# A Fourier mixing layer followed by an expert layer with h·cos(h): five changes to the schedule of a tuned one-core kernel

## The chip, the cores and the metric

The program runs on one core of one Trainium2 chip. The metric is device time in microseconds (us) of one execution; several executions of each kernel are timed on the same chip, in rounds, beside executions of the kernel before. The granted TensorE clock (the share of full speed that the chip let TensorE run at, as the trace records it) is given where it matters.

PE is TensorE (PEld its weight loads), DVE is VectorE, ACT is ScalarE, POOL is GpSimd, SP is the engine whose queue issues most DMAs. PSUM is the memory that PE writes its results to, in banks; SBUF is the memory that the engines work from; DRAM is the memory outside the core.

## The reference

```python
def _attn_ref(x):                       # x: (8, 3008, 256) float32
    X = np.fft.fft(x, axis=1)
    X = np.fft.fft(X, axis=2)
    return X.real.astype(np.float32)

def _moe_ref(x, w_in, w_out):           # x: (24064, 256); 256 -> 2048 -> 256
    h = x @ w_in
    g = h * np.cos(h)
    return (g @ w_out).astype(np.float32)
```

Everything is float32. The kernel folds the 256-channel transform into `w_in` (tables Wc and Ws), uses the symmetries of the 3008-row transform, and computes rows k and 3008-k together: with P the cosine part and Q the sine part, one row needs P+Q and the other P-Q.

Of the kernel before, what the change touches and what calls it, by code (L numbers as in the profile page):

```python
# [69 lines left out]

def _row_consts():

    p = np.arange(128)
    neg = SEQ - 5 - 6 * p
    neg[0] = SEQ - 6
    return np.stack([neg, HALF - 5 - 6 * p], axis=1).astype(np.uint32)
# [3 lines left out]
def kernel(  # L80
# [14 lines left out]
    CC_dr = nc.inline_tensor(_chan_consts(), name="chan_mats")  # L95
    IX_dr = nc.inline_tensor(_row_consts(), name="row_table")
# [25 lines left out]
    ix = cpool.tile([128, 2], U32, tag="ix")  # L122
    nc.sync.dma_start(out=ix, in_=IX_dr.ap())

    def load_x(b):
        L = [
            spool.tile([128, 6 * ND], FP, tag=f"xl{j}", bufs=1, name=f"xl{j}")
            for j in range(4)
        ]

        for j in (2, 1):
            nc.gpsimd.indirect_dma_start(
                out=L[j],
                out_offset=None,
                in_=xflat,
                in_offset=bass.IndirectOffsetOnAxis(ap=ix[:, j - 1 : j], axis=0),
                element_offset=b * SEQ * ND,
            )
        nc.gpsimd.dma_start(out=L[1][0:1, 0 : 5 * ND], in_=xrows(b, SEQ - 5, 1, 1, 5))
        nc.gpsimd.dma_start(out=L[1][0:1, 5 * ND :], in_=xrows(b, 0, 1, 1, 1))  # L140
        nc.sync.dma_start(out=L[0], in_=xrows(b, 0, 6, 128))
        nc.sync.dma_start(out=L[3], in_=xrows(b, HALF, 6, 128))
        return L
# [51 lines left out]
    R4 = cpool.tile([128, NB], FP, tag="R4")  # L195
    Rb4 = cpool.tile([128, NB], FP, tag="Rb4")
# [4 lines left out]
    xe_dr = dpool.tile([NB, 2 * 768], FP, tag="xe", name="xe_dr")  # L201
# [25 lines left out]
    def fold_weights():  # L227
# [14 lines left out]
        nc.scalar.dma_start(out=wx_dr, in_=Ws[127:128, :])  # L242
        with nc.allow_non_contiguous_dma(reason="one row to columns"):
            nc.scalar.dma_start(
                out=wex, in_=wx_dr.rearrange("o (f p) -> p (o f)", p=128)
            )
# [7 lines left out]
    def sum_weights():  # L254
        b11, b12 = w2v[:, 0::2, 0:128], w2v[:, 0::2, 128:256]
        b21, b22 = w2v[:, 1::2, 0:128], w2v[:, 1::2, 128:256]
        gtt(WT[0], b12, b11, ALU.subtract)
        gtt(WT[2], b12, b22, ALU.add)
        gtt(WT[1], b11, WT[2], ALU.subtract)
        gtt(WT[3], WT[1], b21, ALU.add)  # L260
# [4 lines left out]
    def fold_x(L, tt, pieces):  # L265

        ops = {}

# [8 lines left out]
        for j in range(4):  # L277
# [5 lines left out]
            if j in (1, 2):  # L283
# [4 lines left out]
                nc.scalar.copy(out=e, in_=s)  # L288
# [3 lines left out]
            O.append(o)  # L292
        for j in (1, 3):
            ops[f"z{j}", 0] = lambda o=O[j]: pin(
                nc.gpsimd.memset(o[:, 6 * 127 :], 0.0)
            )
# [12 lines left out]
        "c1 e1 o1 c3 e3 o3 c0 e0 E0 o0 O0 c2 e2 E2 EO0 EO1 o2 O2 EO2 z1 EO3 z3".split()  # L309
# [92 lines left out]
    def load_ext():  # L402
        X = state["X"] = []
        with nc.allow_non_contiguous_dma(reason="one channel"):
            for tag, row, n in (
                ("e0", 0, 760),
                ("e2", 748, 760),
                ("o0", HALF, 760),
                ("o2", SEQ - 760, 760),
            ):  # L410
                t = spool.tile([128, 768 if tag[0] == "e" else 763], FP, tag=tag, bufs=1, name="x128")
                nc.sync.dma_start(
                    out=t[0:NB, 0:n],
                    in_=bass.AP(
                        tensor=xt,
                        offset=x.offset + row * ND + 128,
                        ap=[[SEQ * ND, NB], [ND, n], [1, 1]],
                    ),
                )
                X.append(t[0:NB])  # L420

    def fold_ext():
        n = RUN + 1
        X = state["X"]
        XA = spool.tile([128, 768], FP, tag="e1", bufs=1, name="XA")[0:NB]
        XG = spool.tile([128, 768], FP, tag="e3", bufs=1, name="XG")[0:NB]

        gtt(XA[:, 1:n], X[0][:, 1:n], X[3][:, 759 : 759 - RUN : -1], ALU.add)
        gtt(XA[:, 0:1], X[0][:, 0:1], X[0][:, 0:1], ALU.add)
        gtt(XG[:, 0:n], X[1][:, 756 : 756 - n : -1], X[2][:, 0:n], ALU.add)  # L430
        ep, em = X[0], X[1]
        gtt(ep[:, 0:n], XA[:, 0:n], XG[:, 0:n], ALU.add)
        gtt(em[:, 0:n], XA[:, 0:n], XG[:, 0:n], ALU.subtract)
        for i, t in enumerate((ep, em)):
            pin(nc.gpsimd.memset(t[:, n:768], 0.0))
            nc.sync.dma_start(out=xe_dr[:, i * 768 : (i + 1) * 768], in_=t[:, 0:768])
        xe = spool.tile([128, 2, NB, 6], FP, tag="xe", bufs=1, name="xe")
        for i in range(2):
            nc.sync.dma_start(
                out=xe[:, i],  # L440
                in_=xe_dr[:, i * 768 : (i + 1) * 768].rearrange(
                    "b (p m) -> p b m", m=6
                ),
            )
# [20 lines left out]
    def dft_ext_out():  # L465
        ps = state["ext"]
        rx = [
            spool.tile([128, 763], FP, tag=t, bufs=1, name="rx")[0:NB]
            for t in ("o0", "o2")
        ]  # L470
        S = []
        for g in range(4):
            n = NO if g > 1 else NE
            t = spool.tile(
                [128, 763 if g % 2 else 768], FP, tag=("e0", "o1", "e2", "o3")[g], bufs=1, name="sx"
            )[0:NB]
            act(t[:, 0:n], ps[32 * g : 32 * g + NB, 0:n])
            S.append(t)
        for kodd in range(2):
            n = NO if kodd else NE  # L480
            a, b = S[2 * kodd][:, 0:n], S[2 * kodd + 1][:, 0:n]
            gtt(rx[kodd][:, 0:n], a, b, ALU.add)
            o = 1 - kodd
            m = n - 2 * o
            gtt(
                rx[kodd][:, RUN - 1 : RUN - 1 - m : -1],
                a[:, o : o + m],
                b[:, o : o + m],
                ALU.subtract,
            )  # L490
            if not kodd:
                gtt(rx[0][:, RUN : RUN + 1], a[:, 0:1], b[:, 0:1], ALU.subtract)
                nc.sync.dma_start(
                    out=r4_dr.rearrange("o b -> b o"), in_=rx[0][:, RUN : RUN + 1]
                )
            nc.sync.dma_start(
                out=r128_dr[:, kodd * RUN : (kodd + 1) * RUN], in_=rx[kodd][:, 0:RUN]
            )
# [101 lines left out]
    def sum_31(i):  # L600
        S = steps[i]
        outer = S.G[:, 0 : 4 * TW].rearrange("p (f c) -> p f c", f=4)[:, 0::3]
        gtt(
            two(blk(S, 4, 2)),
            blk(S, 2).unsqueeze(1).to_broadcast([128, 2, TW]),
            outer,
            ALU.subtract,
        )
# [136 lines left out]
    def middle_tokens():  # L745
        pm = bank("M")
        for f in range(NF):
            mm(pm[:, f * NB : (f + 1) * NB], Wc[:, f * 128 : (f + 1) * 128], R4, True)
        n = NF * NB
        h = spool.tile([128, 3 * n], FP, tag="hm", bufs=1, name="hm")  # L750
        e, r, h = h[:, 0:n], h[:, n : 2 * n], h[:, 2 * n : 3 * n]
        vtt(
            e.rearrange("p (f b) -> p f b", b=NB),
            Rb4.unsqueeze(1).to_broadcast([128, NF, NB]),
            wex.unsqueeze(2).to_broadcast([128, NF, NB]),
            ALU.mult,
        )
        vtt(h, e, pm[:, 0:n], ALU.add)
        act(r.bitcast(I32), h, bias=0.25, scale=1.0)
        vtt(r, h, r.bitcast(I32), ALU.subtract)  # L760
        sin(r)
        times(h, h, r)
        po = bank("M")
        for f in range(NF):
            mm(
                po[0:NB, 0:ND],
                h[:, f * NB : (f + 1) * NB],
                w2[:, f * ND : (f + 1) * ND],
                f == 0,
                f == NF - 1,  # L770
            )
        ob = spool.tile([128, TW], FP, tag="p1", bufs=1, name="p1")
        act(ob[0:NB], po[0:NB, 0:ND])
# [6 lines left out]
            in_=ob[0:NB],  # L780
        )

# [3 lines left out]
    EO, ops = fold_x(L_first, vtt, 1)  # L786
# [5 lines left out]
    fold_now("c0 e0 o0 c3 e3 o3 c2 e2 E2 o2 O2 c1 e1 E0 EO0")  # L792
# [21 lines left out]
    sum_weights()  # L814

# [8 lines left out]
    for i in range(total):  # L824
        t = i * T
        for dt, fn in (
            (-2.2, ext),
# [3 lines left out]
            (3.1, h_minus),  # L831
            (3.7, k_plus),
            (4.3, k_minus),
            (4.4, r_plus),
            (T + 0.2, r_minus),
            (T + 0.21, sin_plus),
            (T + 0.9, g_plus),
            (T + 1.4, sin_minus),
            (T + 2.0, g_minus),
            (T + 2.6, sum_31),  # L840
            (T + 3.8, sum_2),
            (T + 4.4, sum_4),
# [3 lines left out]
            at(t + dt, lambda fn=fn, i=i: fn(i))  # L846
    for q in range(n_tiles):
        t = (8 * q + 9) * T
        for dt, fn in (
            (1.37, comb_copy),  # L850
# [124 lines left out]
```

## The kernel before: what the change touches

The main loop has 376 steps (47 tiles of 256 columns, 8 steps each). In a step PE multiplies P and then adds Q in the same PSUM bank; between the two, ScalarE copies 2P out, so that h_minus = 2P - (P+Q) can be formed. Then come range reduction (k, r), the sine, the product with h, block sums on GpSimd (sums and differences of 128 x 256 blocks of the result G), and seven products with `w_out`, two steps later. Once a tile, VectorE combines the banks of these products, pA to pD (comb and turn, the boundary sums). Each step begins with `ext`: ScalarE writes the share of channel 128, Rb times a column of `wex`, into the bank H, and PE adds P to it. So the first main-loop matmul, H<-Rr,Wc, needs `wex`. Every PE operation is issued by one helper, `mm`, every two-input VectorE operation by `vtt`, every GpSimd one by `gtt`, and every ScalarE activation by `act`, so these share line numbers in the profile, and the reader goes by tile names.

The order of instructions on each engine is fixed by a list of times (T is 4.8):

```python
for dt, fn in ((-2.2, ext), (0.0, mm_P), (0.9, dbl), (2.17, mm_Q),
               (3.1, h_minus), (3.7, k_plus), (4.3, k_minus), (4.4, r_plus),
               (T + 0.2, r_minus), (T + 0.21, sin_plus), (T + 0.9, g_plus),
               (T + 1.4, sin_minus), (T + 2.0, g_minus),
               (T + 2.6, sum_31), (T + 3.8, sum_2), (T + 4.4, sum_4),
               (2 * T + 0.87, mm_X1), (2 * T + 3.04, mm_X2)): ...   # dbl: E <- 2*P
for dt, fn in ((1.37, comb_copy), (2.65, comb_1), (T + 0.25, comb_2), (T + 1.5, comb_22),
               (T + 2.5, comb_3), (2 * T + 2.6, turn_u), (3 * T + 2.6, turn_v)): ...  # once a tile
```

The opening and the batch loads:

```python
# load_x(b), on GpSimd: two gathers, then row 0 of one of them is mended by two more DMAs
nc.gpsimd.dma_start(out=L[1][0:1, 0 : 5 * ND], in_=xrows(b, SEQ - 5, 1, 1, 5))
nc.gpsimd.dma_start(out=L[1][0:1, 5 * ND :], in_=xrows(b, 0, 1, 1, 1))
# fold_weights(), after eight ScalarE copies: the weight row of channel 128 becomes 16 columns, through DRAM
nc.scalar.dma_start(out=wx_dr, in_=Ws[127:128, :])
nc.scalar.dma_start(out=wex, in_=wx_dr.rearrange("o (f p) -> p (o f)", p=128))
# sum_weights(): four GpSimd sums over 128 x 1024, before the main loop
```

Channel 128 of all eight batches takes a path of its own. Four loads of single elements (4 bytes, rows 1 KB apart) go to 8 SBUF rows, GpSimd folds them on 8 partitions, and the result goes through DRAM to get 128 partitions:

```python
nc.sync.dma_start(out=t[0:NB, 0:n], in_=bass.AP(tensor=xt,
    offset=x.offset + row * ND + 128, ap=[[SEQ * ND, NB], [ND, n], [1, 1]]))      # x4
gtt(XA[:, 1:n], X[0][:, 1:n], X[3][:, 759 : 759 - RUN : -1], ALU.add)            # 8 x 752
... [cut: four more such sums, then SBUF -> xe_dr -> xe]
```

The 8 middle rows (k = 1504) are done in one piece near the end, `middle_tokens()`: 16 matmuls with 8 moving columns, range reduction and sine in a chain, 16 matmuls with 8 stationary columns.

## Time and profile before

| | before |
|---|---|
| time, median of 3 (range) | 2113.97 us (2112.97 to 2116.03) |
| PE busy; mean granted clock | 96%; 0.987 |
| first main-loop matmul starts | 59.4 us |
| an undisturbed step | 4.75 us, 22 PE records, 216 ns apart |
| PE lost against that spacing | about 153 us |

The last row is the measure: take the start-to-start distance of consecutive PE matmul records in the trace, subtract what a record of that many columns takes when PE is not held up at full clock (216 ns for 256 columns, 316 ns for 376), and add up what remains. It holds waits, half clock, and weight loads that are not hidden. Some records of few output columns overlap (the channel-128 products of 376 columns stand 67 ns apart), so for these it is only rough.

The page of the kernel before: span, busy time by engine, the slices of PE and of the granted clock, and the chain that ended last.

```profile
span 2112.5 us, 27423 instructions
...
PE 2029.9 (96%) x8849; PEld 1644.8 (78%) x8849; DVE 1451.1 (69%) x2270; ACT 1445.4 (68%) x2761; POOL 1283.3 (61%) x1421
...
PE   4889999999999999999999999999999999999997
...
PEclk8999999999999999999999999999999999999999
...
PE 69%; ACT 10%; DVE 8%; POOL 7%; issue 3%; DMA 2%; SPq 0%; DVEq 0%; ACTq 0%; POOLq 0%
```

PE bounds the kernel, and almost evenly: the losses lie in the first slices and in many small waits. The waits of the kernel before (engine, line and tile that waited, what for; us in total, times, longest):

```profile
PEld H L212 <- ACT E L224: 62.5, 132, 4.0
...
PEld pB L212 <- POOL G L221: 38.5, 34, 6.3
...
PE pB L212 <- POOL G L221: 26.6, 21, 5.9
POOL xl L139 <- DMA xl<-in_x_dram,ix: 21.8, 7, 11.7
...
DVE e L218 <- ACT e L288: 11.8, 1, 11.8
```

The first line is the 2P copy (tile E): the weight loads of Q wait for it 132 times. By position in the tile, nearly all of these (127) are in steps 2 to 5 of 8, where the tile's boundary sums delay VectorE and so the sines that stand ahead of the copy on ScalarE. The second and third lines are PE waiting for block sums of GpSimd, the fourth is GpSimd waiting for a gather to land before it mends a row, and the last one belongs to the opening, shown next.

The opening of the kernel before, in order of time (start, us, engine, line, operation; in brackets the idle time before and what ended it):

```profile
28.97 0.52 ACT L288 COPY e<-xl 128x6 f32<-128x6 f32 x4 [3.58 <-DMA wx<-Ws]
29.41 0.96 DVE L218 TENSOR_TENSOR e<-e,e 128x768 f32<-128x768 f32 x1 [11.75 <-ACT e L288]
29.98 5.59 POOL L221 TENSOR_TENSOR WT<-w 128x1024 f32<-128x1024 f32 x2 [12.09 <-DMA w<-in_moe_w_out_dram]
30.29 3.09 DVE L218 TENSOR_TENSOR o<-xl 128x762 f32<-128x762 f32 x1
...
43.49 4.11 PE L212 MATMUL pA<-MC,e 128*128 128x377 f32 x6 [18.74 <-issue]
...
59.44 1.13 PE L212 MATMUL H<-Rr,Wc 128*128 128x256 f32 x4 [1.73 <-ACT H L224]
```

ScalarE could not do its small copies until its own DMA issue at 28.5 us had been let through; VectorE idled 11.75 us for them. Then its 762-column folds take 3.0 us while GpSimd sums weights, where they take 0.95 us at other times.

The middle tokens of the kernel before:

```profile
1961.21 4.89 PE L212 MATMUL M<-R,Wc 128*128 128x8 f32 x32
...
1968.00 9.91 PE L212 MATMUL M<-w,hm 128*8 128x256 f32 x32 [1.90 <-DVE hm L584]
...
1977.84 1.13 PE L212 MATMUL pC<-G,WT 128*128 128x256 f32 x4
```

From 1961.2 to 1977.8 us PE does nothing else.

### The profile page before, as it was taken

What the parts mean: (1) busy time and instruction counts of PE and PEld (TensorE: products, weight loads), DVE (VectorE), ACT (ScalarE), POOL (GpSimd) and SP (SyncE); (2) the same over time, 40 slices, a digit from 0 to 9 for tenths busy, and PEclk for the clock granted to TensorE, in tenths of its full rate; (3) what the DMA queues carried; (4) which work ended last, traced back from release to release, by engine and by line L of the source; (5) the groups of instructions that cost most, each with busy time, mean ns of one, the idle gap of its engine ahead of it and who ended that gap; (6) DMA issues with size and microseconds to landing.
All of it is one profiled execution on the core that took longest, in us unless ns stands there. A gap on an engine that the chain in (4) does not pass through costs nothing.

```text
span 2112.5 us, 27423 instructions
## 1 busy us (share of the span) xinstructions
PE 2029.9 (96%) x8849; PEld 1644.8 (78%) x8849; DVE 1451.1 (69%) x2270; ACT 1445.4 (68%) x2761; POOL 1283.3 (61%) x1421
## 2 busy tenths in 40 slices
PE   4889999999999999999999999999999999999997
PEld 2667778887788777888788887878888887888786
DVE  4556667776677766777667766777667776677575
ACT  1656667776677766777677766777667776677575
POOL 2369645884458744687457854578445874455354
PEclk8999999999999999999999999999999999999999
DMA  6912101210012111111101101012010110001001
GB/s 233 61 20 64 33 11 15 57 41 15 13 18 64 25 23 17 31 42 28 26 17 42 38 16 25 11 48 54 7 18 11 25 22 9 13 11 20 11 11 20
DMA packets 252224, 66.81 MB, mean 32 GB/s; under 512 B 242313, under 2 KB 245137, under 8 KB 251569
## 3 DMA queue, kind: packets, MB, share of 16 engines
q1 hardware_dynamic: 247200, 52.42, 14.0%
q0 software_dynamic: 2816, 12.63, 1.8%
q8 instruction: 70, 1.15, 0.2%
q14 instruction: 72, 0.59, 0.1%
q10 hardware_dynamic: 2066, 0.02, 0.1%
HBM read 40.24 MB, written 24.75 MB: 31 GB/s over the span
## 4 chain that ended last, share of the span: by engine, by line
PE 69%; ACT 10%; DVE 8%; POOL 7%; issue 3%; DMA 2%; SPq 0%; DVEq 0%; ACTq 0%; POOLq 0%
PE H L212 31%; PE pD L212 11%; PE pC L212 11%; PE pB L212 10%; PE pA L212 5%; DVE G L218 5%; ACT G L224 5%; POOL G L221 4%; ACT E L224 2%; ACT M L224 2%; POOL o L221 1%; DVE G L584 1%; DMA xl<-in_x_dram,ix 1%; POOL e L221 1%; DVE u L218 1%
## 5 line engine op out<-in xcount | busy, mean ns | idle before, releaser
L221 POOL TENSOR_TENSOR G<-G 128x512 f32<-128x512 f32 x1128 | 1026.3, 910 | 761.2 <-DVE G L584 565.3
L224 ACT ACTIVATE G<-H 128x512 int32<-128x512 f32 x376 | 224.4, 597 | 357.9 <-DVE G L218 357.8
L218 DVE TENSOR_TENSOR G<-H,G 128x512 f32<-128x512 f32 x376 | 260.0, 692 | 246.9 <-ACT G L224 244.8
L584 DVE SCALAR_TENSOR_TENSOR G<-G,M 128x512 f32<-128x512 f32 x376 | 258.3, 687 | 241.9 <-ACT M L224 241.9
L212 PE MATMUL H<-Ir,Ws 127*128 127x256 f32 x1504 | 402.5, 390 | 12.7 <-ACT E L224 8.0
L212 PE MATMUL H<-Rr,Wc 128*128 128x256 f32 x1504 | 392.5, 383 | 1.7 <-ACT H L224 1.7
L212 PE MATMUL pC<-G,WT 128*128 128x256 f32 x1504 | 391.0, 382 | 0.0
L224 ACT ACTIVATE H<-Rb,wex 128x256 f32<-128x256 f32 x752 | 360.0, 479 | 18.9 <-DMA Rb<-r 4.6
L212 PEld LDWEIGHTS H<-Ir,Ws 127*128 127x128 f32 x1504 | 275.1, 190 | 96.4 <-ACT E L224 62.5
L224 ACT ACTIVATE G<-G,halfpi 128x512 f32<-128x512 f32 x376 | 271.5, 722 | 97.7 <-DVE G L218 96.2
L212 PEld LDWEIGHTS pC<-G,WT 128*128 128x128 f32 x1504 | 283.1, 190 | 47.0 <-issue 8.0
L212 PEld LDWEIGHTS H<-Rr,Wc 128*128 128x128 f32 x1504 | 280.5, 190 | 43.1 <-ACT H L224 2.6
L584 DVE SCALAR_TENSOR_TENSOR G<-H,G 128x512 f32<-128x512 f32 x376 | 259.7, 691 | 62.7 <-ACT G L224 62.7
L218 DVE TENSOR_TENSOR G<-E,H 128x512 f32<-128x512 f32 x376 | 254.4, 676 | 58.8 <-PE H L212 48.7
L224 ACT ACTIVATE E<-H 128x512 f32<-128x512 f32 x376 | 218.2, 580 | 111.5 <-PE H L212 111.5
L218 DVE TENSOR_TENSOR M<-G,M 128x512 f32<-128x512 f32 x376 | 257.6, 685 | 0.0
L212 PE MATMUL pB<-G,WT 128*128 128x256 f32 x752 | 227.6, 384 | 26.7 <-POOL G L221 26.6
L224 ACT ACTIVATE M<-M,halfpi 128x512 f32<-128x512 f32 x376 | 245.8, 654 | 0.0
L212 PE MATMUL pD<-G,WT 128*128 128x256 f32 x752 | 228.1, 385 | 0.1
L212 PE MATMUL pD<-G,w 128*128 128x256 f32 x752 | 223.8, 379 | 1.0 <-POOL G L221 1.0
L224 ACT ACTIVATE M<-G 128x512 int32<-128x512 f32 x376 | 224.4, 597 | 0.0
L212 PE MATMUL pA<-G,w 128*128 128x256 f32 x752 | 223.7, 379 | 0.0
(95 smaller groups left out, 1785.3 us busy)
## 6 DMA issues: line engine op xcount, KB each, us to landing
out_dram<-ot SPq DMA_DIRECT2D x504, 32.0 KB
xl<-in_x_dram SPq DMA_DIRECT2D x16, 768.0 KB
MC<-dft_mats SPq DMA_DIRECT2D x4, 1131.0 KB
out_dram<-ot SPq DMA_DIRECT2D x256, 2.0 KB
Rb<-r SPq DMA_DIRECT2D x10, 376.0 KB
w<-in_moe_w_in_dram SPq DMA_DIRECT2D x4, 512.0 KB
w<-in_moe_w_out_dram SPq DMA_DIRECT2D x1, 2048.0 KB
out_dram<-ot SPq DMA_DIRECT2D x64, 28.0 KB
```

The costliest lines, as they stand in the source:

```text
L212: nc.tensor.matmul(out_, lhsT=lhsT, rhs=rhs, start=start, stop=stop, skip_group_check=True)
L218: pin(nc.vector.tensor_tensor(out=o, in0=a, in1=b, op=op))
L221: pin(nc.gpsimd.tensor_tensor(out=o, in0=a, in1=b, op=op))
L224: pin(nc.scalar.activation(out=o, in_=i, func=func, **kw))
L584: nc.vector.scalar_tensor_tensor(out=o, in0=h, scalar=TWO_PI, in1=c, op0=ALU.mult, op1=ALU.mult)
```

## The change

Five intents: (1) clear the opening (DMAs of wx and wex from ScalarE's queue to GpSimd's, the first row's mend as a copy, weight sums in pieces inside the loop); (2) channel 128 laid out on 128 partitions by DMA alone, without the fold on 8 partitions, and batch folds spread over more steps; (3) batch loads without the two mending DMAs, except for the last batch; (4) the 2P copy ahead of the sines, the boundary sums where VectorE idles; (5) middle tokens in 32-column tiles, in nine pieces. The core of the diff:

```diff
             (0.9, dbl),
             (2.17, mm_Q),
-            (3.1, h_minus), (3.7, k_plus), (4.3, k_minus), (4.4, r_plus),
-            (T + 0.2, r_minus), (T + 0.21, sin_plus), (T + 0.9, g_plus),
-            (T + 1.4, sin_minus), (T + 2.0, g_minus),
-            (T + 2.6, sum_31), (T + 3.8, sum_2), (T + 4.4, sum_4),
+            (3.55, h_minus), (4.2, k_plus), (4.8, k_minus), (T + 0.2, r_plus),
+            (T + 0.9, r_minus), (T + 1.5, sin_plus), (T + 2.2, g_plus),
+            (T + 2.21, sin_minus), (T + 2.9, g_minus), (T + 2.91, sum_1),
+            (T + 3.6, sum_3), (T + 4.4, sum_2), (2 * T + 0.3, sum_4),
 [cut: boundary sums at 1.45, 4.2, T + 1.0, T + 1.1, T + 1.2, 2T + 1.0, 3T + 1.0]
-        nc.gpsimd.dma_start(out=L[1][0:1, 0 : 5 * ND], in_=xrows(b, SEQ - 5, 1, 1, 5))
-        nc.gpsimd.dma_start(out=L[1][0:1, 5 * ND :], in_=xrows(b, 0, 1, 1, 1))
+        [first row by a copy out=L[1][0:1, 5 * ND :], in_=L[0][0:1, 0:ND]: ScalarE for
+         the first batch, GpSimd for the others; one DMA stays for the last batch]
-        nc.scalar.dma_start(out=wx_dr, in_=Ws[127:128, :])
+        nc.gpsimd.dma_start(out=wx_dr, in_=Ws[127:128, :])           [wex likewise]
-    xe_dr = dpool.tile([NB, 2 * 768], FP, tag="xe", name="xe_dr")
+    xe_dr = dpool.tile([4, NB, 768], FP, tag="xe", name="xe_dr")
+    def load_ext(j):
+        first, step = ((0, 1), (SEQ, -1), (HALF, -1), (HALF, 1))[j]
+        def copy(s0, s1, row, step):
+            nc.sync.dma_start(
+                out=xe_dr[j, :, s0:s1],                               # DRAM to DRAM
+                in_=bass.AP(tensor=xt, offset=x.offset + row * ND + 128,
+                    ap=[[SEQ * ND, NB], [step * ND, s1 - s0], [1, 1]]))
+    def get_ext():
+        for j in range(4):
+            nc.sync.dma_start(out=xs[:, j],
+                in_=xe_dr[j].rearrange("b (p m) -> p b m", m=6))
     def fold_ext():                              [five sums of 8 x 753 become:]
+        gtt(xs[:, 0::2], xs[:, 0::2], xs[:, 1::2], ALU.add)          # 128 x 96
+        gtt(xe[:, 0], xs[:, 0], xs[:, 2], ALU.add)                   # 128 x 48
+        gtt(xe[:, 1], xs[:, 0], xs[:, 2], ALU.subtract)
+    def mid_mm():                                          [in place of middle_tokens()]
+        for n, (W, R) in enumerate(((Wc, R4), (Ws, Rx4))):
+            wv = W.rearrange("p (j g a) -> p g j a", g=4, a=32)
+            for g in range(4):
+                mm(pm[32 * g : 32 * g + 32, :], R, wv[:, g], n == 0, n == 1)
+ [cut: mid_h, mid_r, mid_g, mid_out, mid_copy, mid_pick, mid_store, one a step]
-    at(1 * T, load_ext)
-    at(9 * T + 2.7, fold_ext)
+    for j in range(4):
+        at((2 * j - 1) * T + 0.2, lambda j=j: load_ext(j))
+    at(8 * T, get_ext)
+    at(11 * T + 1.35, fold_ext)
-        f0 = s0 + (16 if b == 1 else 8)          [batch folds: steps f0 to f1]
-        f1 = s0 + 28
+        f0 = max(7, s0 - 1)
+        f1 = s0 + 38
```

## The prediction

> **What bounds it now.** TensorE: busy 2030 of 2112 us (96%, the page's first part); the chain that ended last is 69% PE. In an undisturbed step (timeline, 1953 to 1958 us) PE repeats every 4.75 us without a gap; its 22 records stand 216 ns apart. Start-to-start distances of PE records beyond that spacing add up to about 150 us, in five places:
>
> 1. Opening: the first main-loop matmul starts at 59.4 us. ScalarE sits behind its own DMA issue (wx, wex: until 28.5 us) and holds the small copies, so VectorE idles 11.75 us; then VectorE folds with two SBUF inputs take 3.0 us in place of 0.95 while GpSimd sums w2 (30 to 41.6 us).
> 2. 119 to 221 us: GpSimd does the channel-128 fold (8 partitions, 1.8 us each) and a crowded first fold; PE waits for block sums, longest 6.1 us, in all about 19 us, plus 3 us at half clock.
> 3. Batch loads: GpSimd waits for a gather to land before it issues two fix-up DMAs (21.8 us of waits); PE loses some 12 us at 400 to 1470 us.
> 4. Tile boundaries: weight loads of the Q product wait for the 2P copy (132 waits, 62.5 us), all in steps 2 to 5 of a tile of 8, some 0.9 us a tile: about 40 us.
> 5. Middle tokens: PE is taken from 1961.2 to 1977.8, 16.6 us, partly at half clock.
>
> **What the change does.** (1) DMAs leave ScalarE's queue, row fix-up becomes a ScalarE copy, w2 sums go into loop steps. Once that copy is through (about 26 us, after the last weight copy), three folds of 0.95 us remain: first DFT near 29 instead of 43.5, first loop matmul near 46. The Trainium skill (SBUF — State Buffer, Who interferes with whom) says VectorE operations with two SBUF inputs contend with GpSimd reads; here 0.95 against 3.0 us. About -13 us. (2) channel 128 is laid out by DMA, folds at 96 elements a partition, first fold spread over 31 steps: -17. (3) fix-up for the last batch only: -10. (4) copy ahead of sines, sums where VectorE idles: -33; slack stays about 0.4 us at boundaries. (5) 32-column tiles: existing channel-128 DFT records of 376 columns stand 67 ns apart, not 315, so four column tiles overlap; estimated 4 to 5 us of PE, interleaved: -12. Comb_3 earlier: -3. Added: one more GpSimd op a step (0.73 us for 256 columns, total about 3, as before), w2 sums in the first steps.
>
> Sum about -88; I give back some 7 for new waits, because slack of PSUM banks in DFT steps shrinks.
>
> **What would make it wrong.** The 24,576 four-byte DRAM-to-DRAM writes: the old loads took 48 us (60 to 108 us). If writes are slower, or queued behind the DFT matrices (landing near 34 us), GpSimd stalls at step 11 and PE with it, 10 to 30 us. Software descriptors for wex could delay the first step. Boundary sums in a row could make block sums late each tile (0.2 us each is 10 us).
>
> **Check.** First Rr product near 46 us; PE busy share 98%; waits of H on E under 15 us; PE on GpSimd under 15 us; middle-token matmuls interleaved, no 0.5 clock near 1960; VectorE folds 0.95 us.
>
> Predicted 2032 us, 8 in 10 between 2008 and 2068. Chances: faster by over 2% 0.90, within 0.09, slower 0.01.

## More of the kernel before

The four loads of channel 128 in the SP queue of the kernel before:

```profile
55.91 37.35 SPq L412 DMA_DIRECT2D x<-in_x_dram  x4
```

## The result, and the profile after

| | before | after |
|---|---|---|
| time, median (range, runs) | 2115.0 us (2112.97 to 2116.95, 4) | 2103.18 us (2101.5 to 2104.2, 4) |
| ratio | | 0.9943 (95%: 0.9926 to 0.9961) |
| PE lost, as defined above | 153 us | 132 us, of which 82.4 us in one wait |
| first main-loop matmul | 59.4 us | 48.05 us |

A ratio is the mean time of one kernel's runs over the mean of the other's runs of the same rounds, so it is not quite the ratio of the medians quoted. Gains in us are differences between the medians of a kernel and of the kernel before in the same rounds (the latter between 2113.8 and 2116.0 us). The kernel is 0.6% faster, a difference clear of noise but under 2%; I had said 4%, and the time lies outside my range.

The two figures of PE lost are not quite alike: the changed kernel's middle tokens use records that overlap, and the measure charges them at full width. With every kind of record counted at what it takes when nothing holds it, I find about 146 us before, 139 us after and, for the mended kernel told below, 46 us; the distance between the last two is 93 us either way.

The page after:

```profile
span 2099.5 us, 27859 instructions
...
PE 1980.4 (94%) x8838; PEld 1651.8 (79%) x8838; DVE 1402.6 (67%) x2276; ACT 1433.3 (68%) x2730; POOL 1337.9 (64%) x1842
...
PE   6921999999999999999999999999999999999997
...
PEclk9865999999999999999999999999999999999999
...
PE 86%; SPq 6%; DMA 2%; DVE 2%; POOL 1%; ACT 1%; issue 1%; another core or an unknown queue 0%; DVEq 0%; POOLq 0%; ACTq 0%
```

PE busy went down by 49.5 us, but the span by only 13: slices 3 and 4 are nearly empty and their clock is down to 0.5 to 0.6. By the clock records of the trace it was 0.5 from 121 to 203 us, and also from 46 to 63 us. The chain names the culprit's queue, "SPq 6%", where the kernel before had 0%. The waits after:

```profile
POOL xs L237 <- DMA xs<-xe_dr: 83.0, 1, 83.0
...
PE H L228 <- POOL xe L237: 82.2, 1, 82.2
...
PEld pB L228 <- POOL G L237: 14.1, 38, 1.0
...
PEld H L228 <- ACT E L240: 7.5, 30, 1.5
...
PE pB L228 <- POOL G L237: 2.6, 8, 0.6
```

The last three lines answer to the first three of before: the 2P copy costs 7.5 us where it cost 62.5, and PE's waits for block sums are 14.1 and 2.6 us where they were 38.5 and 26.6. What the change aimed at there, it got. The first two lines are new: GpSimd waited 83.0 us for tile xs, which comes from DRAM (xe_dr), and PE 82.2 us for GpSimd. The SP queue's own timeline says why it came late (the time given to an issue holds its standing in the queue):

```profile
25.11 0.84 SPq L431 DMA_DIRECT2D xe_dr<-in_x_dram  x1
35.99 34.89 SPq L149 DMA_DIRECT2D xl<-in_x_dram  x1
...
71.41 78.09 SPq L431 DMA_DIRECT2D xe_dr<-in_x_dram  x4
149.61 47.08 SPq L451 DMA_DIRECT2D xs<-xe_dr  x4
```

L431 are the four loads of channel 128 (in five pieces), L149 a batch load, L451 the read into xs. The batch load takes 34.9 us to issue, because the queue ahead of it is full of 4-byte packets, and the loads after it take 78.1 us, where all four took 37.4 us in the kernel before. The opening after:

```profile
25.40 0.39 ACT L314 COPY xl<-xl 1x256 f32<-1x256 f32 x1
...
25.90 0.95 DVE L287 TENSOR_TENSOR e<-xl 128x762 f32<-128x762 f32 x1
...
28.88 3.84 PE L228 MATMUL pA<-MC,e 128*128 128x377 f32 x6 [4.01 <-DVE e L287]
...
47.01 0.99 ACT L240 ACTIVATE H<-Rb,wex 128x256 f32<-128x256 f32 x2 [6.08 <-DMA wex<-wx]
...
48.05 1.22 PE L228 MATMUL H<-Rr,Wc 128*128 128x256 f32 x2 [5.79 <-ACT H L240]
```

The first two lines and the first DFT matmul at 28.88 us are as predicted (26 and 29). The first loop matmul had been expected near 46; it came at 48.05, because the ScalarE instruction ahead of it waited 6.08 us for wex, whose DMA ran among the 4-byte packets and landed 17.1 us after its issue (9.6 us in the mended kernel below). The middle tokens no longer stop PE; the next two fences, of before and then of after, show two stretches of time each. Their columns are the stretch, its length, the busy us (and instructions) of PE, PEld, DVE, ACT and POOL, the granted clock, the DMA share and GB/s:

```profile
60.00:230.00 170.00, 149.82 (x644) 119.97 (x643) 102.09 (x159) 108.72 (x208) 116.67 (x132) 0.95 0.38 33
...
1890.00:1990.00 100.00, 97.65 (x434) 76.70 (x433) 63.82 (x103) 64.03 (x124) 45.38 (x51) 0.95 0.08 11
```

```profile
60.00:230.00 170.00, 85.66 (x377) 67.28 (x376) 53.66 (x88) 57.70 (x110) 61.02 (x92) 0.75 0.73 21
...
1890.00:1990.00 100.00, 98.72 (x470) 82.36 (x470) 73.83 (x119) 75.59 (x145) 56.11 (x79) 1.00 0.09 15
```

The first line of each pair is the region of the stall: 86 us of PE work where there had been 150, at a mean clock of 0.75 in place of 0.95. The second is the region of the middle tokens (their first piece in the changed kernel, at 1886 us, lies just ahead of it): the clock is 1.00 there and no longer 0.95.

To see the packets themselves I counted the DMA records of the SP queue with a size of 4 bytes. In the kernel before, the four loads (about 6,080 packets each) took 9.6, 11.3, 13.2 and 14.0 us, 435 to 635 packets per us. In the changed one (6,144 each) they took 43.4, 43.5, 33.1 and 34.4 us, 141 to 186 packets per us, and the last ended at 185 us. The first two shared their time with the matrices and a batch load; but from 90 to 118 us and from 118 to 185 us, when the records show hardly a packet but these, they went at 164 and 183 per us. Two of the four read rows in falling order (the second and third), and they are not the slow ones as a group. So the direction is not the cause.

### The profile page after: what moved, and what is told of

Read it like the earlier page. It is cut to its first block, busy times and chain, and to the rows that moved or that the text cites. A ratio compares the mean times of both kernels' runs of the same rounds, so it can differ in the third digit from the quotient of the medians.

```text
span 2099.5 us, 27859 instructions
## 1 busy us (share of the span) xinstructions
PE 1980.4 (94%) x8838; PEld 1651.8 (79%) x8838; DVE 1402.6 (67%) x2276; ACT 1433.3 (68%) x2730; POOL 1337.9 (64%) x1842
## 4 chain that ended last, share of the span: by engine, by line
PE 86%; SPq 6%; DMA 2%; DVE 2%; POOL 1%; ACT 1%; issue 1%; another core or an unknown queue 0%; DVEq 0%; POOLq 0%; ACTq 0%
PE H L228 36%; PE pB L228 14%; PE pC L228 14%; PE pD L228 14%; PE pA L228 7%; SPq L431 4%; SPq L451 2%; POOL G L237 1%; DMA wex<-wx 1%; DVE G L594 1%; DMA w<-in_moe_w_in_dram 1%; ACT G L240 1%; DVE G L234 0%; DMA wx<-Ws 0%
## 5 line engine op out<-in xcount | busy, mean ns | idle before, releaser
L237 POOL TENSOR_TENSOR G<-G 128x256 f32<-128x256 f32 x1504 | 1080.9, 729 | 629.0 <-DVE G L594 532.0
L240 ACT ACTIVATE E<-H 128x512 f32<-128x512 f32 x376 | 224.4, 597 | 351.9 <-PE H L228 348.5
L228 PE MATMUL H<-Ir,Ws 127*128 127x256 f32 x1504 | 389.5, 381 | 1.5 <-ACT E L240 1.5
L240 ACT ACTIVATE H<-Rb,wex 128x256 f32<-128x256 f32 x752 | 360.4, 479 | 25.4 <-DMA wex<-wx 6.1
L228 PEld LDWEIGHTS H<-Ir,Ws 127*128 127x128 f32 x1504 | 283.6, 190 | 46.2 <-ACT E L240 7.5
L228 PE MATMUL pB<-G,w 128*128 128x256 f32 x752 | 223.7, 379 | 0.0
```

Source lines behind the costliest of these rows:

```text
L228: nc.tensor.matmul(out_, lhsT=lhsT, rhs=rhs, start=start, stop=stop, skip_group_check=True)
L237: pin(nc.gpsimd.tensor_tensor(out=o, in0=a, in1=b, op=op))
L240: pin(nc.scalar.activation(out=o, in_=i, func=func, **kw))
```

## The experiments

The theory after the result, called W: 4-byte writes to DRAM are what is slow; everything else in the prediction holds. Rivals: R, the reads are slow (768 a row, queued behind the DFT matrices); L, a narrower form of W, that only neighbouring 4-byte writes in DRAM are slow; and that some of the other parts failed too, hidden by the stall.

### Rows in SBUF (e2)

```diff
-                out=xe_dr[j, :, s0:s1],
+                out=xr[:, s0:s1],            # xr: 8 rows of one SBUF tile, partitions 32j to 32j+7
 ... in get_ext, ahead of the reads:
+            for j in range(4):
+                nc.sync.dma_start(out=xe_dr[j], in_=state["xr"][32 * j : 32 * j + NB, 0:768])
```

> The changed kernel with one difference: the four loads of channel 128 read the same 4-byte elements in the same order, but write them to 8 SBUF rows; the rows then go to DRAM in 3 KB runs, and from there on as in the change. Theory W (4-byte writes to DRAM are what is slow): the 4-byte packets go back to about 490 per us as in the kernel before (against 188 per us in the changed one), the folds of channel 128 no longer wait, PE is not idle at 117 us, time about 2018 us (2099.5 less the 82.4 us stall, give or take 5). Rival R (the reads: 768 a row, two of the four downwards, behind the DFT matrices): still about 190 packets per us, stall over 50 us, time over 2065 us. The result is right.

Measured: correct, 2010.42 us (2008.93 to 2011.73), ratio to before 0.9509 (0.9493 to 0.9525), 92.8 us below the changed kernel (91.6 by the gains) and below the 2018, give or take 5, that I had expected. It is called the mended kernel from here on. The loads took 20.9, 14.2, 12.3 and 12.9 us. Its SP queue:

```profile
35.96 15.88 SPq L149 DMA_DIRECT2D xl<-in_x_dram  x1
...
52.37 25.49 SPq L435 DMA_DIRECT2D xr<-in_x_dram  x4
77.96 17.02 SPq L455 DMA_DIRECT2D xe_dr<-xr  x4
95.03 2.34 SPq L457 DMA_DIRECT2D xs<-xe_dr  x4
```

xs is read at 95 us and not at 150, in time for the fold; the wait of GpSimd on xs is gone from its list. The gain is more than the 82.4 us wait: the first loop matmul also starts at 43.96 in place of 48.05 us, and the half clock from 46 to 63 us and after the stall is gone (from 33 us on the clock is 1.0 until the last matmul). PE lost 39 us in all, against 132, a difference of 93. Theory R falls: the reads are the same, in the same order.

### Elements 512 bytes apart in DRAM (e3)

```diff
-    xe_dr = dpool.tile([4, NB, 768], FP, tag="xe", name="xe_dr")
+    xe_dr = dpool.tile([4, NB, 768, 128], FP, tag="xe", name="xe_dr")
-                out=xe_dr[j, :, s0:s1],
+                out=xe_dr[j, :, s0:s1, 0:1],
 [get_ext then reads 24 times 1,024 single elements]
```

> The changed kernel with the 4-byte elements written 512 bytes apart in DRAM in place of side by side; get_ext then reads single elements, so the total is longer and is not the point. Theory L (neighbouring elements fall into one line and their writes wait for each other): during the loads the packets go up to 350 to 490 per us. Theory W (every 4-byte write to DRAM is slow): 170 to 210 per us, as in the changed kernel. The time would be over 2110 us under W, because get_ext adds 24,576 single reads.

Measured: correct, 2013.06 us, a single run. The loads took 16.8, 12.2, 10.3 and 10.0 us (366 to 615 packets per us). I had expected over 2110 us under W: W in its broad form falls. A 4-byte write to DRAM is not slow by itself; L holds so far. Even the 24,576 single reads added to get_ext took only until about 100 us.

### get_ext without its dependency (e4)

```diff
                 nc.sync.dma_start(
                     out=xs[:, j],
-                    in_=xe_dr[j].rearrange("b (p m) -> p b m", m=6),
+                    in_=bass.AP(tensor=xt, offset=x.offset + j * 1024,
+                        ap=[[6, 128], [768, NB], [1, 6]]),          # wrong data on purpose
```

> The changed kernel, but get_ext reads runs of 24 bytes of the input x, not what the loads wrote, so nothing waits for the loads, which still run in the background (wrong result on purpose). If the wait of the GpSimd fold on the loads is the whole of what my prediction missed: 2017 us plus or minus 6, PE wait on GpSimd for xe under 20 us. The SP queue issues in order, though: get_ext stands behind the fourth load's issue, about 150 us; if the queue, not the dependency, holds the fold, the stall stays at 60 us or more and the time over 2070 us.

Measured: wrong result; 2105.51 us, ratio 0.9956 (0.9936 to 0.9976). The stall stays, to within a microsecond:

```profile
73.61 79.15 SPq L431 DMA_DIRECT2D xe_dr<-in_x_dram  x4
152.80 43.72 SPq L451 DMA_DIRECT2D xs<-in_x_dram  x4
```

```profile
POOL xs L237 <- DMA xs<-in_x_dram: 82.7, 1, 82.7
```

So it is enough that get_ext stands behind the loads in the queue. Taking away the data dependency alone mends nothing.

### Four spacings in one kernel (e8)

```diff
+    xe_dr = [dpool.tile([NB, w, e], FP, tag=f"xe{j}", name="xe_dr")
+        for j, (w, e) in enumerate(((768, 64), (768, 16), (768, 4), (800, 1)))]
-                out=xe_dr[j, :, s0:s1],
+                out=xe_dr[j][:, s0:s1, 0:1],
```

> The changed kernel, each of the four loads with another spacing of its 4-byte writes in DRAM: 256, 64, 16 and 4 bytes in this order, the last with rows padded to 800 elements so that the destination is no single run. If neighbouring writes that share a line of 64 bytes wait for each other (theory L), the first two run at 450 to 650 packets per us and the 4-byte one at 170 to 220; 16 bytes lies between. If instead the single-run shape of the destination was what made the changed kernel slow, the last load is as fast as the others, over 450 per us. The total time is not the point (reads of single elements by get_ext are added); right result.

Measured: correct, 2050.95 us, a single run (the total was not the point). By load, counted as above:

| bytes between elements | 256 | 64 | 16 | 4, rows padded |
|---|---|---|---|---|
| load took, us | 15.7 | 14.6 | 23.8 | 38.1 |
| packets per us | 390 | 420 | 258 | 161 |

The first two shared their time with other loads (matrices, the batch), so they are lower bounds. The spacing falls with the order of the loads here, but the order is not the cause: in e3, with one spacing for all, the later loads were the faster ones. The last load is as slow as in the changed kernel although its destination is not one run: the shape of the destination is not the cause, the nearness of the elements is. That writes which fall close together wait for each other would fit, but no run shows the mechanism: why they are slow stays open.

### The parts one by one

Three kernels take one part each of the change into the kernel before; the edits are those of the diff above.

New step order alone (e5):

```diff
 [kernel before, with the lists of step and tile times, sum_1 and sum_3, and the
  places of the DFT copies of the change]
```

> The kernel before with the new order of a step alone (copy of 2P ahead of sines, split block sums, tile sums at the new places, DFT copies moved), all else as before. My prediction gave this part 36 us (33 and 3): 2076 to 2082 us, and waits of H weight loads on the 2P copy under 15 us against 62.5. Rival: it shares its gain with the GpSimd folds that this kernel still crowds into 12 or 20 steps, and gains under 20 us: over 2094 us.

Measured: correct, 2073.63 us, ratio 0.9807 (0.979 to 0.9823): 40.2 us. Better than my 36, and just below the range that I had given. The waits on the 2P copy are gone from the top of its list (5.8 us), but GpSimd costs more than before (38.5 and 26.6 us there):

```profile
PEld pB L212 <- POOL G L221: 57.4, 77, 4.4
PE pB L212 <- POOL G L221: 33.1, 27, 4.0
```

Opening and loads alone (e10):

```diff
 [kernel before, with load_x, fold_x, sum_weights(i) in steps, and the queue of wx and wex of the change]
```

> The kernel before with the new opening and the new row fix-up of the batch loads alone (DMAs of wx and wex on GpSimd, first row by a ScalarE copy, w2 sums in loop steps). My prediction: 13 us from the opening and 10 from the loads, 2091 us (2086 to 2097), with the first Rr product near 46 us and VectorE folds of 0.95 us. Rival: batch folds that stay crowded into 12 and 20 steps keep most of the GpSimd waits at the loads, so that 13 us or less is gained: 2101 us or more.

Measured: correct, 2088.7 us, ratio 0.9875 (0.9853 to 0.9897): 25.4 us against my 23. The first loop matmul starts at 43.9 us here, where the channel-128 loads do not disturb wex.

Middle tokens alone (e6):

```diff
 [kernel before, with mid_mm to mid_store, R4 and Rx4 of 32 columns, and their nine steps]
```

> The kernel before with the middle tokens of the change alone (32-column tiles, spread over nine steps). My prediction: 12 us less, about 2102 us (2099 to 2105); the 16.6 us in which PE did nothing else, at 1961 us, and the half clock there are gone. Rival: the old stretch let GpSimd and VectorE catch up, and the new pieces take PSUM banks from the steps, so less than 5 us is gained: over 2109 us.

Measured: correct, 2106.53 us (2105.59 to 2112.11), ratio 0.9965 (0.9938 to 0.9991): 7.6 us, with an interval that still held my 12. So I took the part out of the mended kernel as well.

Old middle tokens in the mended kernel (e13):

```diff
 [kernel of "rows in SBUF", with middle_tokens(), R4, Rb4 and spread4() of the kernel before]
```

> The mended kernel (rows in SBUF) with the old middle tokens put back. Alone on the kernel before, the new ones gained 7.6 us, interval about 2 to 13. By PE time I count 16.6 us against 4.7 us of the new pieces: 11.9 us, so 2022 us here (2020 to 2024) if the stall is pure loss; if catching up after the stall takes part of it back, 2018 us or less.

Measured: correct, 2017.81 us (2017.24 to 2019.62), ratio 0.9545 (0.9532 to 0.9558), 7.4 us above the median of the mended kernel (7.0 by the gains, 103.4 and 96.4 us). It was run at another time. Both experiments agree on 7 to 8 us, and my 12 falls. The step periods of PE show where the rest is. A tile with neither middle tokens nor products of the 3008-row transform takes 38.19 us in these kernels. The old tokens add 15.9 us to one tile (54.12 us). The new ones add 6.6 and 1.4 us to two tiles (44.82 and 39.55 us), 8.0 in all, of which the new PE pieces themselves (1.86, 0.70, 1.87, 0.21, 0.55 and 0.31 us) are 5.5. The old piece did not give time back afterwards (the tile after it takes 38.19 us); the new pieces are dearer than I took them for, and their VectorE and ScalarE instructions push others. In one step, for example, the residue of the middle tokens stands among the boundary sums on VectorE, and PE starts 0.6 us late for a boundary sum.

The change with the old channel-128 path (e7):

```diff
 [changed kernel, with load_ext, fold_ext, dft_ext_out and their times of the kernel before]
-        f0 = max(7, s0 - 1)
-        f1 = s0 + 38
+        f0 = 16 if b == 1 else s0 - 1       # the old loads use the folds' tiles until then
+        f1 = 28 if b == 1 else s0 + 38
```

> The changed kernel with the channel-128 path of the kernel before (4-byte loads into SBUF rows, fold on 8 partitions) and the first batch's folds in steps 16 to 28, all else as changed. If the parts add up: 2113.8 less 40 (measured for the step order), 23 and 12 is 2039 us, give or take 6; the distance to 2010 us is then what the new channel-128 path is worth when its writes don't stall it: about 28 us, more than the 17 that I predicted. If it is near 2012 the new path is worth nothing.

Measured: correct, 2027.7 us, ratio 0.9585 (0.9563 to 0.9606). Its gain is 86.4 us, where that of the mended kernel is 103.4, so the new path, with the first batch's folds spread over more steps as it allows, is worth 17.0 us once its writes do not stall it, give or take some 6 by the intervals of the two ratios. That agrees with what I had predicted (to the tenth by luck), and the 28 that I expected here falls. But then the sum of the three parts (40.2 + 25.4 + 7.6 = 73.2 us) is 13 short of the 86.4 us that this kernel gains. By the intervals of the four ratios, taken as independent, this distance is known to some 9 us only.

Old folds and loads (e11):

```diff
 [the kernel just told]
-        l0 = max(0, s0 - 8)
+        l0 = 0 if b == 1 else s0 + 1
-        f0 = 16 if b == 1 else s0 - 1
-        f1 = 28 if b == 1 else s0 + 38
+        f0 = 16 if b == 1 else s0 + 8
+        f1 = s0 + 28
```

> The changed kernel with the old channel-128 path and also the old places of the batch loads (step 1 of a batch, not 8 steps earlier) and folds (steps 8 to 28, not -1 to 38). The sum of the parts measured one by one, 40 + 25 + 8 us, falls 13 us short of what the kernel with only the old channel-128 path gained (86 us). If the wider spread of folds and the earlier loads, which I left out of my prediction for all batches but the first, are those 13 us, this runs at 2041 us, give or take 4, with PE waits on GpSimd of over 10 us more than there. If the parts help one another otherwise, it stays near 2028 us.

Measured: correct, 2032.62 us, ratio 0.961 (0.9595 to 0.9625), 83.4 us below before. The spread of the folds and the early loads are worth some 3 us of the 13 (the two intervals overlap), and my expectation falls. The other 10, if they are real, would be parts helping one another. PE's loss ahead of the product that needs block sum 2 points to where: 30.7 us in the kernel before, 39.8 with the new step order alone, 20.3 with the new opening and loads alone, and 21.9 here with both. The new order alone loses 9 us there, because it leaves GpSimd less slack; with the loads' mending DMAs gone, it loses next to nothing. This is read from traces, not isolated by a run of its own: that it is the cause is not shown.

### Beyond the mend

First-row copy on VectorE (e9):

```diff
 [kernel of "rows in SBUF"]
-            (nc.scalar.copy if eng is nc.vector else eng.tensor_copy)(
+            eng.tensor_copy(
-    fold_now("x1 c0 e0 o0 c3 e3 o3 c2 e2 E2 o2 O2 c1 e1 E0 EO0")
+    fold_now("c0 e0 o0 c3 e3 o3 c2 e2 E2 o2 O2 x1 c1 e1 E0 EO0")
```

> The mended kernel (rows in SBUF) with one more edit: the first row's 1x256 copy on VectorE, between its folds, not on ScalarE behind the eight weight copies. ScalarE did that copy at 25.4 us in the changed kernel while the gathered rows had landed by 17 us, so VectorE idled 4.8 us and PE 4.2 us, followed by matmuls at half clock. If that wait is on the critical path, the first DFT starts near 25 in place of 29 us and the time is 4 to 7 us lower than with rows in SBUF alone: 2004 to 2007 us. If something else holds the first steps (wex, or the DFT matrices landing by 25 us), the gain is under 2 us: 2009 us or more.

Measured: correct, 2013.7 us, ratio 0.9519 (0.9506 to 0.9532): no gain (102.3 us below before, against 103.4). The first DFT did start at 24.48 in place of 28.9 us, but the first loop matmul at 43.88, as before the edit. The timeline shows the new wait:

```profile
34.62 0.46 POOL L237 TENSOR_TENSOR WT<-WT,w 128x128 f32<-128x128 f32 x1
34.71 6.51 DVE L287 TENSOR_TENSOR e<-e,e 128x768 f32<-128x768 f32 x1
35.03 0.86 POOL L237 TENSOR_TENSOR WT<-w 128x128 f32<-128x128 f32 x2
...
42.84 0.99 ACT L240 ACTIVATE H<-Rb,wex 128x256 f32<-128x256 f32 x2 [6.67 <-DVE Rb L234]
...
43.88 1.65 PE L228 MATMUL H<-Rr,Wc 128*128 128x256 f32 x3 [6.39 <-ACT H L240]
```

A fold with two SBUF inputs, 0.95 us elsewhere, takes 6.51 us, from 34.7 to 41.2 us, and GpSimd runs weight sums of 0.45 us in that whole time (the last of them is stretched to 1.05 us). Two explanations that I had written down (wex, the matrices) are not it.

First folds ahead of the sums (e12):

```diff
 [kernel just told]
-    fold_now("o1 O0 EO2 z1")
+    fold_now("z1 z3 o1 O0 EO2 EO1 EO3")
-    fold_now("EO1 EO3 z3")
-                nc.gpsimd.memset(o[:, 6 * 127 :], 0.0)
+                eng.memset(o[:, 6 * 127 :], 0.0)
```

> The kernel of the VectorE copy again, with the last two folds of the first batch moved ahead of the w2 sums (and two small memsets from GpSimd to VectorE). In that run one fold with two SBUF inputs took 6.51 us, from 34.7 to 41.2 us, while GpSimd ran w2 sums without a gap, and PE waited 6.55 us. If this contention gave the gain back, all first folds take 0.95 us here, the first Rr product starts at 41 us or a little before (wex landed 9.6 us after its issue, about 39.5 us) in place of 43.9, and the time is 2 to 5 us below rows in SBUF alone: 2006 to 2009 us on a baseline of 2114. If the start stays near 44 us, wex or the matrices hold it and the contention only covered that.

Measured: correct, 2007.59 us (2005.14 to 2009.46), ratio 0.9492 (0.9479 to 0.9505). All first folds take 0.95 us, and the first loop matmul starts at 38.99 us, 5 us earlier; ScalarE then waits 2.85 us for wex. The two memsets move in the same edit, so the 5 us belong to both together. The median is 2.8 us below rows in SBUF, but the two intervals overlap, so whether it is the faster of the two in time stays open. They were run at other times. The mean clock of its first 60 us is 0.91 against 0.97, which eats part of the 5 us. Both beat the kernel before by some 5% and the changed kernel by some 4.5%.

## Why the prediction was wrong, point by point

- **Bound and losses.** PE bounds the kernel, and the five places of loss were the right ones. PE's loss went from 153 to 39 us in the mended kernel (146 to 46 by the recount), and PE is busy for 98% of its span, as predicted.
- **Step order (predicted 33, and 3 for the earlier comb_3).** 40.2 us alone. Right, a little low.
- **Opening and loads (13 and 10).** 25.4 us together. Right. In the changed kernel itself the opening gave 11.4 us (59.4 to 48.05), because the channel-128 packets delayed wex.
- **Contention of folds with GpSimd.** The Trainium skill (SBUF — State Buffer, Who interferes with whom) says that a VectorE instruction with two SBUF inputs contends with a GpSimd one that reads SBUF. The trace of before agrees (0.95 against 3.0 us), and e9 shows it again (6.51 us).
- **Middle tokens (12).** 7.0 and 7.6 us. The term was too large: I took 4 to 5 us for the new pieces, they add 8.0. The reason for them holds: the Trainium skill (TensorEngine Tiling (Array Packing), Tiling Modes) says that tiles operate independently, and here eight records of 512 columns in four column tiles took 0.88 us, 110 ns each; the skill's page does not say what they do to the other engines.
- **Channel 128 (17).** 17.0 us, give or take 6, but only once the writes are mended.
- **New waits (7 to give back).** They did not show: without the stall, the whole change gains 103.4 us, more than my sum of 88. The surplus over the terms as measured one by one (40.2, 25.4, 7.0 and 17.0 us) is the distance of some 13 us told above, which I had not foreseen.
- **The step that failed** is the cost of the 4-byte writes to DRAM, which stands in "What would make it wrong": "The 24,576 four-byte DRAM-to-DRAM writes: the old loads took 48 us (60 to 108 us). If writes are slower, or queued behind the DFT matrices (landing near 34 us), GpSimd stalls at step 11 and PE with it, 10 to 30 us." The place, the engine and the step are right. I kept it out of the sum, as if the writes went at the old loads' pace, and sized it at a third or less. In its place the runs showed that packets of 4 bytes written side by side in DRAM go at 141 to 186 per us, where those of the old loads into SBUF went at 435 to 635, so that the loads end at 185 and not near 90 us, and cost 92.8 us: 82.4 in the wait and 4.1 in the later start; of the other 6, by PE's records, some 4 fall between 46 and 64 us, where the clock is 0.5, and near 2 after the stall, which PE also leaves at 0.5 (until 203 us). The Trainium skill (TensorE: Matmul & The Clock Gate, Part 1) describes half clock after an idle window; here the clock fell to 0.5 at 121 us, 4 us after PE had stopped, and the changed kernel's clock averages 0.75 from 60 to 230 us, against 1.00 in the mended one. Without that one term the prediction would have been 2032 against 2010 us, inside its range.

## What to carry to other kernels

When a change moves a scattered gather from SBUF to DRAM, its writes have to be priced afresh: here the time of the old loads said nothing about them. Gather single elements into SBUF, or space them in DRAM (at 64 bytes they went at 420 per us or more, side by side at 161), and look at what stands behind them in the same queue, because everything there waits too, dependent or not. And a risk that is written down with a size belongs in the sum, with its chance; one that can stop PE for a whole queue's length deserves the largest range.

## What the Trainium skill lacked or had wrong

- DMA: Bandwidth & Descriptors (Specifications) says that transfers under 512 B are below line rate and do read-modify-write. Taken as the reason of the stall, that would make every 4-byte write to DRAM slow alike. The runs show 366 to 615 packets per us for 4-byte writes 512 bytes apart, no slower than 4-byte writes to SBUF (294 to 500 in e2), 420 or more at 64 bytes apart, but 258 at 16 and 141 to 186 at 4. The page lacks that nearness of the writes decides.
- The same page (Issuing engines are not separate DMA queues) says that DMAs of all engines share 16 DMA engines, which agrees: 6,144-byte packets of a batch gather from GpSimd's queue, 0.24 us each when alone, took 0.6 to 6.2 us on average in stretches of 5 us beside the 4-byte writes. It says that the time to issue is usually small beside the DMA itself; here one batch load stood 34.9 us in its issue on SP behind such packets.
- SBUF — State Buffer (Summary: rules for kernel authors) says that of the two the second to issue is blocked until the first finishes. In e9 a VectorE fold that began during one GpSimd sum of 0.45 us took 6.51 us in place of 0.95, through 14 further sums; the page lacks that a chain of sums without gaps can hold VectorE for longer than one of them.
